# Output weights converted where they are used, and weight splits in front of the products

## The chip, the cores and the metric

One core of a Trainium2 chip runs the whole program. The metric is the device time of one execution in microseconds (us); the median of several executions is compared. TensorE (PE) multiplies, with its weight loads (PEld) on a row of their own, VectorE (DVE), ScalarE (ACT) and GpSimd (POOL) do the rest, and SyncE (SP) issues most transfers.

## The reference

The program is three stages on 2304 tokens (4 batches of 576) with 512 features.

```python
kv = np.einsum('bhsd,bhse->bhde', k, v); out = np.einsum('bhsd,bhde->bhse', q, kv)
x = out / sqrt(mean(out * out, -1) + 1e-6) * g_norm          # linear attention, heads joined
e = argmax(x @ w_gate); gate = softmax(x @ w_gate)[e]        # one of 8 experts, capacity 576
x = gate * (maximum(x @ w1[e], 0) @ w2[e])                   # w1: 512x1024, w2: 1024x512
h = maximum(maximum(x @ m2w1, x @ m2w2), x @ m2w3)           # maxout, 512x768 each
out = h @ w_out                                              # 768x512
```

The four matrices of the maxout stage arrive as doubles (64 bits); everything else is float32.

## The kernel before, in words

**Products.** Every float32 operand of a large product is split into a high part `hi` and a remainder `lo`, and a product is three matmuls (`mm3`, L765 to L767): hi·hi, hi·lo, lo·hi. Here `hi` is written by ScalarE and `lo` by VectorE. For a weight tile of 128x512 this pair stands in `split_next` (L297 on ScalarE, L298 on VectorE); `stream[0]` counts the tiles, and the tile of the w1 chunk f of expert r is t = 16r + f. Weights come into four `raw` buffers of 512 KB, two tiles each; the transfer of a later chunk is asked for when the second half of an earlier one has been split (`raw_upto`).

**Experts.** The experts run one after the other. For expert r, eight groups `gemm1_f` (f = 0 to 7) give `ph`, of which ScalarE writes the high part of `h` (L788, relu) and VectorE its remainder (L789). Then four groups `gemm2_dc` give `py`; the group walks through h 0 to 7 in order, so its first group needs the last `h` some 3 us after it begins. Row counts fall from 374 (second expert) to 284 (eighth); the first expert has 324. In the first expert VectorE also does the ranking of the experts between the products (`rk_gen`).

**Doubles.** Float32 copies of the maxout matrices are made during the experts, in blocks of 128x256 doubles. One `dbl_step` stores block i-3 (transfer queue of ScalarE), loads block i+3 (SyncE) and converts block i in `dbl_round`: two ScalarE instructions (L912, L913), three of VectorE (L914, L915, L917), two of GpSimd (L918, L919). There are 48 blocks: 36 of the three maxout matrices, 12 of the output matrix. `DBL1[r]` lists the f after which a step stands, `DBL2[r][dc]` how many stand after a `gemm2_dc`. Steps past the last block only store. The float32 copies go to DRAM and come back as `raw` chunks.

**Maxout.** The tokens are taken in six blocks of 384 (j). For each of six column chunks c, three products `pa` of 12 matmuls each use six PSUM buffers in turn (three per c). ScalarE copies `pa[0]` to `m` (L1096), VectorE takes the maximum with the other two (L1097, L1098), ScalarE writes the high part of `g` (L1099) and VectorE its remainder (L1100). Then three groups `pz` of 18 matmuls multiply g of c = 0 to 5 with the tiles `wot(c)` of the output matrix. At j = 0 the last maxout tiles (c = 0) and the six output tiles (two each at c = 1, 2, 3) are still to be split; `split_next` stands behind the matmuls of c and ahead of `m`.

**Order.** The schedule is manual: each engine carries out its instructions in the order in which the code writes them.

Of the kernel before, what the change touches and what calls it, by code (L numbers as in the profile page):

```python
# [21 lines left out]
B, H, S, D = 4, 8, 576, 64  # L22
NT, DM, NE, FF, F2 = B * S, H * D, 8, 1024, 768
# [17 lines left out]
def kernel(  # L41
# [21 lines left out]
    ct = dram.tile([NT, 3], F32, name="ct")  # L63

    doubles = []
    if m2w1.dtype == mybir.dt.int64:
        d64 = [m2w1, m2w2, m2w3, m2wo]
        m2w1, m2w2, m2w3 = (dram.tile([DM, F2], F32, name=f"m2w{a}") for a in range(3))
        m2wo = dram.tile([F2, DM], F32, name="m2wo")
        for cb in range(F2 // 256):  # L70
            for a, dst in enumerate([m2w1, m2w2, m2w3]):
                for rb in range(NDC):
                    doubles.append((d64[a], dst, rb, cb))
        for rb in range(NC2):
            for cb in range(DM // 256):
                doubles.append((d64[3], m2wo, rb, cb))
    ND = len(doubles)
# [155 lines left out]
    sp, act = ENG.SP, ENG.Activation  # L233
    NRAW = NE * 8 + 12
    NW = 20
# [12 lines left out]
    def raw_dma(i):  # L248
# [16 lines left out]
        if j < 9:  # L265
# [3 lines left out]
        j -= 9  # L269
        return nc.sync.dma_start(raw.rearrange("p (c f) -> p c f", c=2),  # L270
                                 m2wo[j * 256:(j + 1) * 256, :].rearrange("(c p) f -> p c f", p=128))

# [7 lines left out]

    def split_next(n=1, eng=None):
        for _ in range(n):
            i, half = divmod(stream[0], 2)
            stream[0] += 1
            if i >= NRAW:
                continue
            raw = raws[i]
            t_ = wtile(2 * i + half)
            wt[2 * i + half] = t_
            if i < NE * 8 + 9:  # L290
                src = raw.rearrange("p (c f) -> p c f", c=4)[:, :, half * 128:(half + 1) * 128]
# [610 lines left out]
    def dbl_round(i):  # L902

        if i < ND:
            t_ = dt_[i]
            w_ = dpool[0].tile([128, 256], F32, tag="dw", bufs=6, name=f"dw{i}")
            dt_[i, "w"] = w_
            lo, hi = t_[:, :, 0], t_[:, :, 1]  # L910
            wi = w_.bitcast(I32)
            nc.scalar.activation(out=w_, in_=hi.bitcast(F32), func=AF.Copy, scale=2.0 ** -112)  # L912
            nc.scalar.activation(out=lo.bitcast(F32), in_=lo.bitcast(U32), func=AF.Copy, scale=2.0 ** -52)  # L913
            nc.vector.tensor_scalar(out=wi, in0=wi, scalar1=3, scalar2=None, op0=ALU.logical_shift_left)  # L914
            nc.vector.scalar_tensor_tensor(out=wi, in0=hi, scalar=-2 ** 31, in1=wi,  # L915
                                           op0=ALU.bitwise_and, op1=ALU.bitwise_or)
            nc.vector.tensor_scalar(out=hi, in0=wi, scalar1=-2 ** 23, scalar2=None, op0=ALU.bitwise_and)  # L917
            nc.gpsimd.tensor_tensor(out=lo.bitcast(F32), in0=hi.bitcast(F32), in1=lo.bitcast(F32), op=ALU.mult)  # L918
            nc.gpsimd.tensor_tensor(out=w_, in0=lo.bitcast(F32), in1=w_, op=ALU.add)  # L919

# [107 lines left out]

    DBL1 = [(), (3, 5), (3, 5), (1, 3, 5), (1, 4), (1, 4), (1, 4), (1, 3, 5, 7)]
    DBL2 = [(0, 0, 0, 0), (1, 1, 1, 2), (1, 2, 1, 2), (1, 2, 1, 2), (1, 1, 1, 2)] + [(1, 1, 1, 1)] * 2 + [(2, 2, 0, 0)]  # L1030
    for r in range(NE):
# [10 lines left out]
        if r == NE - 1:  # L1042
            ct_load()
        for f in range(NFC):
            gemm1_f(r, f)
            if r == 0:
                for _ in range(9 if f == 0 else 6):
                    next(rk_gen, None)
                if f == 3:
# [32 lines left out]
    for j in range(NYB):  # L1082
        h2 = []
        for c in range(NC2):
# [36 lines left out]
    with tc.If(flag):  # L1121
        spill(ctx, tc, dict(
            er_f=er_f, nr_f=nr_f, mr_f=mr_f, trir=trir, capf=capf, e2304=e2304, slot=slot, ident=ident, g2=g2,
            xs=xs, ct=ct, w1=w1, w2=w2, m2w=m2w, m2wo=m2wo, out=out))


def spill(ctx, tc, a):
# [3 lines left out]
    with ExitStack() as st:  # L1131
# [164 lines left out]
```

## Time and profile before

| | |
|---|---|
| median of 3 executions (lowest, highest) | 647.64 us (646.8, 650.21) |
| the profiled execution: its time, its span | 650.49 us, 648.6 us |
| TensorE busy | 619.0 us (95%), mean granted clock 0.982 |
| VectorE, ScalarE, GpSimd busy | 338.0, 274.0, 196.5 us |
| attention and routing / experts / maxout, from the timeline | 0 to 88 / 88 to 337 / 337 to 649 us |

The three boundaries are the first matmul of the first expert and the first of the maxout part on TensorE. Busy time of an engine other than TensorE matters only where TensorE waits for it.

### The profile page before, as it was taken

To read this page: it belongs to the slowest core of one execution; us is meant where nothing else is said; L and a number is where in the kernel's file an instruction comes from. 1 tells how busy PE (TensorE), PEld (TensorE's weight loads), DVE (VectorE), ACT (ScalarE), POOL (GpSimd) and SP (SyncE) were. 2 spreads that over 40 slices of the span, in tenths; PEclk is the share of its full clock that TensorE was granted. 3 is DMA by queue.
4 is the path that set the end of the run, shared out by engine and by line. 5 is a ranking of instruction groups with operands and counts; after the bars stand their busy time and mean duration, and the time that the engine had idled before them with its cause. 6 is when DMAs were issued, how large, how long until landed. Compare 5 with 4: busy or idle time off the path is not lost.

```text
span 648.6 us, 11278 instructions
## 1 busy us (share of the span) xinstructions
PE 619.0 (95%) x4113; PEld 593.8 (92%) x4113; DVE 338.0 (52%) x718; ACT 274.0 (42%) x629; POOL 196.5 (30%) x278
## 2 busy tenths in 40 slices
PE   8898988999999999999999999999999999999992
PEld 8788888999998989999999989989989989989992
DVE  2546867886889888888985322222322222221220
ACT  1655864856575857576753221121121121121110
POOL 3247643122858585857530010010010010001001
PEclk9978998999999999999999999999999999999997
DMA  8999347866888788888962000000000000000000
GB/s 226 282 297 297 122 164 236 256 234 214 246 249 276 235 264 254 259 251 255 275 184 65 1 34 16 1 33 17 1 33 17 0 17 33 0 17 33 1 18 35
DMA packets 81373, 88.35 MB, mean 136 GB/s; under 512 B 15017, under 2 KB 70825, under 8 KB 81314
## 3 DMA queue, kind: packets, MB, share of 16 engines
q1 hardware_dynamic: 68448, 66.64, 35.5%
q0 software_dynamic: 5952, 14.65, 6.5%
q10 hardware_dynamic: 6914, 6.30, 2.8%
q8 instruction: 34, 0.56, 0.4%
q14 instruction: 25, 0.20, 0.1%
HBM read 71.80 MB, written 15.76 MB: 135 GB/s over the span
## 4 chain that ended last, share of the span: by engine, by line
PE 63%; DVE 9%; DMA 4%; issue 3%; ACT 2%; ACTq 0%; POOL 0%; SPq 0%; DVEq 0%; POOLq 0%
PE pa L767 12%; PE pa L766 12%; PE pa L765 12%; PE py L766 4%; DVE w L298 4%; PE py L767 4%; PE py L765 4%; PE pz L1110 4%; PE pz L1109 4%; PE pz L1111 4%; DVE h L789 2%; DMA d<-in_moe_w_dram 2%; PE ph L767 2%; PE ph L766 2%; PE ph L765 2%
## 5 line engine op out<-in xcount | busy, mean ns | idle before, releaser
L766 PE MATMUL pa<-ys,w 128*128 128x384 f32 x432 | 144.3, 334 | 0.0
L765 PE MATMUL pa<-ys,w 128*128 128x384 f32 x432 | 144.3, 334 | 0.0
L767 PE MATMUL pa<-ys,w 128*128 128x384 f32 x432 | 144.3, 334 | 0.0
L298 DVE TENSOR_TENSOR w<-raw,w 128x512 fp32r<-128x512 f32 x152 | 114.6, 783 | 26.7 <-ACT w L297 23.1
L1114 POOL DMA_INDIRECT out_dram<-o,ctab x18 | 17.5, 973 | 286.9 <-ACT o L1113 276.7
L1097 DVE TENSOR_TENSOR m<-pa,m 128x384 f32<-128x384 f32 x36 | 20.1, 558 | 137.6 <-PE pa L767 137.6
L297 ACT ACTIVATE w<-raw 128x512 fp32r<-128x512 f32 x152 | 89.5, 624 | 4.8 <-DMA raw<-in_moe_w_dram 4.8
L766 PE MATMUL py<-h,w 128*128 128x324 f32 (+7 forms) x256 | 81.4, 318 | 7.2 <-DVE h L789 7.2
L1099 ACT ACTIVATE g<-m 128x384 fp32r<-128x384 f32 x36 | 18.9, 526 | 150.0 <-DVE m L1098 150.0
L766 PEld LDWEIGHTS pa<-ys,w 128*128 128x128 f32 x432 | 81.1, 188 | 0.2
L765 PEld LDWEIGHTS pa<-ys,w 128*128 128x128 f32 x432 | 81.1, 188 | 0.2
L767 PEld LDWEIGHTS pa<-ys,w 128*128 128x128 f32 x432 | 81.1, 188 | 0.0
L765 PE MATMUL py<-h,w 128*128 128x324 f32 (+7 forms) x256 | 80.2, 313 | 0.0
L767 PE MATMUL ph<-xt,w 128*128 128x324 f32 (+7 forms) x256 | 79.6, 311 | 0.5 <-DVE w L298 0.5
L765 PE MATMUL ph<-xt,w 128*128 128x324 f32 (+7 forms) x256 | 79.3, 310 | 0.6 <-ACT xt L667 0.6
L767 PE MATMUL py<-h,w 128*128 128x324 f32 (+7 forms) x256 | 79.8, 312 | 0.0
L766 PE MATMUL ph<-xt,w 128*128 128x324 f32 (+7 forms) x256 | 79.4, 310 | 0.2 <-DVE xt L668 0.2
L766 PEld LDWEIGHTS py<-h,w 128*128 128x128 f32 x256 | 48.8, 191 | 10.8 <-DVE h L789 10.6
L918 POOL TENSOR_TENSOR d<-d 128x256 f32<-128x256 f32 x48 | 30.7, 640 | 75.5 <-issue 18.2
L765 PEld LDWEIGHTS ph<-xt,w 128*128 128x128 f32 x256 | 48.3, 189 | 0.8 <-ACT xt L667 0.8
L767 PEld LDWEIGHTS ph<-xt,w 128*128 128x128 f32 x256 | 48.3, 189 | 0.8 <-DVE w L298 0.8
L765 PEld LDWEIGHTS py<-h,w 128*128 128x128 f32 x256 | 48.9, 191 | 0.0
(247 smaller groups left out, 1034.1 us busy)
## 6 DMA issues: line engine op xcount, KB each, us to landing
raw<-in_moe_w_dram SPq DMA_DIRECT2D x64, 512.0 KB, 5.4
d<-in_moe_w_dram SPq DMA_DIRECT2D x36, 256.0 KB, 5.2
m2w<-dw ACTq DMA_DIRECT2D x36, 128.0 KB, 4.5
raw<-m2w SPq DMA_DIRECT2D x9, 512.0 KB, 4.6
k<-in_k_dram SPq DMA_DIRECT2D x8, 512.0 KB, 8.7
v<-in_v_dram SPq DMA_DIRECT2D x8, 512.0 KB, 9.2
q<-in_q_dram SPq DMA_DIRECT2D x8, 512.0 KB, 8.5
d<-in_moe_w_out_dram SPq DMA_DIRECT2D x12, 256.0 KB, 5.2
```

The source lines that it names most:

```text
L297: nc.scalar.activation(out=hi, in_=src, func=AF.Copy)
L298: (eng or nc.vector).tensor_tensor(out=lo, in0=src, in1=hi.bitcast(F32), op=ALU.subtract)
L765: nc.tensor.matmul(po, lhi, rhi, start=first, stop=False)
L766: nc.tensor.matmul(po, lhi, rlo, start=False, stop=False)
L767: nc.tensor.matmul(po, llo, rhi, start=False, stop=last)
L918: nc.gpsimd.tensor_tensor(out=lo.bitcast(F32), in0=hi.bitcast(F32), in1=lo.bitcast(F32), op=ALU.mult)
L1097: nc.vector.tensor_tensor(out=m_, in0=pa[1][:, :YB], in1=m_, op=ALU.max)
L1099: nc.scalar.activation(out=t_[:, 0], in_=m_, func=AF.Copy)
L1109: nc.tensor.matmul(po, h_[:, 0], w_[:, 0], start=c == 0, stop=False)
L1110: nc.tensor.matmul(po, h_[:, 0], w_[:, 1], start=False, stop=False)
L1111: nc.tensor.matmul(po, h_[:, 1], w_[:, 0], start=False, stop=c == NC2 - 1)
L1114: nc.gpsimd.indirect_dma_start(out=out, out_offset=IndirectOffsetOnAxis(ap=ctab[:, jt, 0:1].bitcast(I32), axis=0), in_=o_, in_offset=None)
```

## The change

**Output matrix.** Its 12 blocks leave the list of doubles. `raw` now takes 128x512 doubles of it directly, six chunks instead of three. In `split_next` each of the six output tiles is converted first (`to_float32`, the same seven instructions on 512 columns, on a tile `wd`) and then split, at j = 0: one maxout chunk's two tiles at c = 0, two output tiles at c = 1, one each at c = 2 to 5. For a rarely needed branch (`spill`, skipped by a flag in these runs) the split tiles, not float32, are stored to DRAM.

**Schedule of the doubles.** `DBL1` and `DBL2` place 39 steps (36 blocks and three that only store) where 51 stood.

**First expert.** `split_next` stands ahead of `gemm1_f`: four tiles at f = 0, two at f = 1 to 4, none at 5, and one behind the group at f = 6 and 7. Before it stood behind the group, two tiles at f = 0 to 5.

```diff
-        d64 = [m2w1, m2w2, m2w3, m2wo]
+        d64 = [m2w1, m2w2, m2w3]
-        for rb in range(NC2):
-            for cb in range(DM // 256):
-                doubles.append((d64[3], m2wo, rb, cb))
...
-    NRAW = NE * 8 + 12
+    NRAW = NE * 8 + 9 + NC2
...
+    def to_float32(lo, hi, w_):
+        wi = w_.bitcast(I32)
+        nc.scalar.activation(out=w_, in_=hi.bitcast(F32), func=AF.Copy, scale=2.0 ** -112)
+        nc.scalar.activation(out=lo.bitcast(F32), in_=lo.bitcast(U32), func=AF.Copy, scale=2.0 ** -52)
+        nc.vector.tensor_scalar(out=wi, in0=wi, scalar1=3, scalar2=None, op0=ALU.logical_shift_left)
+        nc.vector.scalar_tensor_tensor(out=wi, in0=hi, scalar=-2 ** 31, in1=wi,
+                                       op0=ALU.bitwise_and, op1=ALU.bitwise_or)
+        nc.vector.tensor_scalar(out=hi, in0=wi, scalar1=-2 ** 23, scalar2=None, op0=ALU.bitwise_and)
+        nc.gpsimd.tensor_tensor(out=lo.bitcast(F32), in0=hi.bitcast(F32), in1=lo.bitcast(F32), op=ALU.mult)
+        nc.gpsimd.tensor_tensor(out=w_, in0=lo.bitcast(F32), in1=w_, op=ALU.add)
...
+                src = xgs[0].tile([128, H, D], F32, tag="xn", name=f"wd{i}").rearrange("p h d -> p (h d)")
+                words = raw.bitcast(I32).rearrange("p (f c) -> p f c", c=2)
+                to_float32(words[:, :, 0], words[:, :, 1], src)
             nc.scalar.activation(out=hi, in_=src, func=AF.Copy)
-            (eng or nc.vector).tensor_tensor(out=lo, in0=src, in1=hi.bitcast(F32), op=ALU.subtract)
+            nc.vector.tensor_tensor(out=lo, in0=src, in1=hi.bitcast(F32), op=ALU.subtract)
...
-    DBL1 = [(), (3, 5), (3, 5), (1, 3, 5), (1, 4), (1, 4), (1, 4), (1, 3, 5, 7)]
-    DBL2 = [(0, 0, 0, 0), (1, 1, 1, 2), (1, 2, 1, 2), (1, 2, 1, 2), (1, 1, 1, 2)] + [(1, 1, 1, 1)] * 2 + [(2, 2, 0, 0)]
+    DBL1 = [(), (3, 5, 7), (1, 3, 5, 7), (1, 3, 5, 7), (3, 7), (7,), (), (1, 3, 5)]
+    DBL2 = [(0,) * 4] + [(1,) * 4] * 3 + [(1,) * 4, (1, 1, 1, 0), (1, 1, 1, 0), (0,) * 4]
...
         for f in range(NFC):
+            if r == 0:
+                split_next(4 if f == 0 else 2 if f < 5 else 0)
             gemm1_f(r, f)
...
-            split_next(1 if r else 2 if f < 6 else 0)
+            split_next(1 if r or f > 5 else 0)
...
             if j == 0:
-                split_next(2)
+                split_next(2 if c < 2 else 1)
```

**Where the instructions stand.** ScalarE in the maxout part, from the first block's `m` on. Before, two splits (`w` from `raw`) stand between `g` of one chunk and `m` of the next:

```order
L1096 ACTIVATE m_4864<-pa_4819 128x384
L1099 ACTIVATE g_4865<-m_4864 128x384
L297 ACTIVATE w_4910<-raw_4734 128x512
L297 ACTIVATE w_4913<-raw_4734 128x512
L1096 ACTIVATE m_4916<-pa_4871 128x384
L1099 ACTIVATE g_4917<-m_4916 128x384
L297 ACTIVATE w_4962<-raw_4779 128x512
L297 ACTIVATE w_4965<-raw_4779 128x512
L1096 ACTIVATE m_4968<-pa_4923 128x384
L1099 ACTIVATE g_4969<-m_4968 128x384
```

Now the two converting instructions and the split of each output tile stand there, and the split reads `wd`, which GpSimd finishes:

```order
L312 ACTIVATE w_4726<-raw_4570 128x512
L312 ACTIVATE w_4729<-raw_4570 128x512
L1105 ACTIVATE m_4734<-pa_4687 128x384
L1108 ACTIVATE g_4735<-m_4734 128x384
L283 ACTIVATE wd_4781<-raw_4604 128x512
L284 ACTIVATE raw_4604<-raw_4604 128x512
L312 ACTIVATE w_4780<-wd_4781 128x512
L283 ACTIVATE wd_4795<-raw_4647 128x512
L284 ACTIVATE raw_4647<-raw_4647 128x512
L312 ACTIVATE w_4794<-wd_4795 128x512
L1105 ACTIVATE m_4808<-pa_4741 128x384
L1108 ACTIVATE g_4809<-m_4808 128x384
```

So `m` of chunk 1 stands behind two whole conversions, and `m` of each chunk from 2 on behind one.

VectorE in the fifth expert (314 rows), from the fourth `h` of the first product to the last one. Before (the `dw` and `d` instructions are the conversion of one block):

```order
L789 SCALAR_TENSOR_TENSOR h_3279<-ph_3266,h_3279 128x314
L298 TENSOR_TENSOR w_3282<-raw_3029,w_3282 128x512
L789 SCALAR_TENSOR_TENSOR h_3300<-ph_3287,h_3300 128x314
L298 TENSOR_TENSOR w_3303<-raw_3110,w_3303 128x512
L914 TENSOR_SCALAR dw_3309<-dw_3309 128x256
L915 SCALAR_TENSOR_TENSOR dw_3309<-d_3158,dw_3309 128x256
L917 TENSOR_SCALAR d_3158<-dw_3309 128x256
L789 SCALAR_TENSOR_TENSOR h_3332<-ph_3319,h_3332 128x314
L298 TENSOR_TENSOR w_3335<-raw_3110,w_3335 128x512
L789 SCALAR_TENSOR_TENSOR h_3355<-ph_3342,h_3355 128x314
L298 TENSOR_TENSOR w_3358<-raw_3155,w_3358 128x512
L789 SCALAR_TENSOR_TENSOR h_3376<-ph_3363,h_3376 128x314
```

Now, from the fifth `h` on:

```order
L808 SCALAR_TENSOR_TENSOR h_3289<-ph_3276,h_3289 128x314
L313 TENSOR_TENSOR w_3292<-raw_3110,w_3292 128x512
L808 SCALAR_TENSOR_TENSOR h_3310<-ph_3297,h_3310 128x314
L313 TENSOR_TENSOR w_3313<-raw_3110,w_3313 128x512
L808 SCALAR_TENSOR_TENSOR h_3333<-ph_3320,h_3333 128x314
L313 TENSOR_TENSOR w_3336<-raw_3155,w_3336 128x512
L808 SCALAR_TENSOR_TENSOR h_3354<-ph_3341,h_3354 128x314
L313 TENSOR_TENSOR w_3357<-raw_3155,w_3357 128x512
L285 TENSOR_SCALAR dw_3365<-dw_3365 128x256
L286 SCALAR_TENSOR_TENSOR dw_3365<-d_3113,dw_3365 128x256
L288 TENSOR_SCALAR d_3113<-dw_3365 128x256
```

The conversion that stood among the last four `h` now stands behind the last one. Ahead of that stretch and behind the fourth expert's last `gemm2_dc` group, the number of conversions falls from three to two.

ScalarE at the begin of the first expert, before (`TENSOR_LOAD` and `ISA` read three offsets into registers; `w` are weight splits, `h` the relu of a product):

```order
L297 ACTIVATE w_1291<-raw_697 128x512
L297 ACTIVATE w_1294<-raw_697 128x512
L1024 TENSOR_LOAD po_i
L1024 ISA x2
L1024 TENSOR_LOAD po_i
L1024 ISA x2
L1024 TENSOR_LOAD po_i
L1024 ISA x2
L788 ACTIVATE h_1369<-ph_1356 128x324
L297 ACTIVATE w_1385<-raw_699 128x512
L297 ACTIVATE w_1388<-raw_699 128x512
L788 ACTIVATE h_1406<-ph_1393 128x324
```

And now:

```order
L312 ACTIVATE w_1291<-raw_697 128x512
L312 ACTIVATE w_1294<-raw_697 128x512
L1031 TENSOR_LOAD po_i
L1031 ISA x2
L1031 TENSOR_LOAD po_i
L1031 ISA x2
L1031 TENSOR_LOAD po_i
L1031 ISA x2
L312 ACTIVATE w_1356<-raw_699 128x512
L312 ACTIVATE w_1359<-raw_699 128x512
L312 ACTIVATE w_1364<-raw_701 128x512
L312 ACTIVATE w_1367<-raw_701 128x512
```

The four splits moved ahead of the first `h`, but stay behind the register loads.

## Rows read from the trace of the kernel before

**Rows 1.** The page: busy time by engine.

```profile
PE 619.0 (95%) x4113; PEld 593.8 (92%) x4113; DVE 338.0 (52%) x718; ACT 274.0 (42%) x629; POOL 196.5 (30%) x278
```

**Rows 2.** Waits of the weight loads (PEld), first expert, 94 to 124 us: total, times, longest.

```profile
PEld py L766 <- DVE h L789: 2.6, 2, 1.4
PEld ph L767 <- DVE w L298: 0.8, 1, 0.8
```

**Rows 3.** The same for the fourth to eighth expert, 192 to 337 us.

```profile
PEld py L766 <- DVE h L789: 7.4, 10, 1.3
```

**Rows 4.** The same for the second to eighth expert, 124 to 337 us.

```profile
PEld py L766 <- DVE h L789: 8.0, 11, 1.3
```

**Rows 5.** Busy by stretch (PE, PEld, DVE, ACT, POOL); then granted clock, DMA share, GB/s.

```profile
94.00:110.00 16.00, 13.44 (x84) 12.46 (x83) 15.08 (x49) 8.63 (x19) 5.28 (x4) 0.99 0.60 183
110.00:113.00 3.00, 3.00 (x13) 3.00 (x13) 0.00 (x0) 1.35 (x5) 0.00 (x0) 0.50 0.97 282
337.10:374.55 37.45, 37.45 (x219) 37.45 (x218) 16.92 (x30) 12.25 (x25) 0.00 (x0) 1.00 0.11 35
```

**Rows 6.** Timeline of ScalarE, start of the first expert: start, length, instruction, idle before.

```profile
88.10 1.14 ACT L297 ACTIVATE w<-raw 128x512 fp32r<-128x512 f32 x2
93.42 0.44 ACT L788 ACTIVATE h<-ph 128x324 fp32r<-128x324 f32 x1 [4.18 <-PE ph L767]
```

**Rows 7.** Timeline of VectorE, first expert: first and last two of eight h.

```profile
93.90 0.50 DVE L789 SCALAR_TENSOR_TENSOR h<-ph,h 128x324 fp32r<-128x324 f32 x1 [2.59 <-ACT h L788]
...
108.88 0.89 DVE L789 SCALAR_TENSOR_TENSOR h<-ph,h 128x324 fp32r<-128x324 f32 x2
```

**Rows 8.** Timeline of TensorE, begin of the first expert's second product.

```profile
107.81 0.42 PE L766 MATMUL py<-h,w 128*128 128x324 f32 x1 [1.16 <-DVE h L789]
...
109.42 0.54 PE L766 MATMUL py<-h,w 128*128 128x324 f32 x1 [0.90 <-DVE h L789]
...
110.29 0.47 PE L766 MATMUL py<-h,w 128*128 128x324 f32 x1
```

**Rows 9.** Timeline of VectorE near the end of the fourth expert's first product.

```profile
208.07 1.44 DVE L298 TENSOR_TENSOR w<-raw,w 128x512 fp32r<-128x512 f32 x1
```

**Rows 10.** Source line L297, split, ScalarE: minimum/median/maximum ns, first and last start.

```profile
L297 ACT ACTIVATE w<-raw x152: 613/623/650, 84.5 to 357.6; 128x512 fp32r<-128x512 f32 x152
```

**Rows 11.** Source line L298, split, VectorE, the same columns.

```profile
L298 DVE TENSOR_TENSOR w<-raw,w x152: 675/691/1441, 85.2 to 358.3; 128x512 fp32r<-128x512 f32 x152
```

**Rows 12.** Source line L912, conversion, ScalarE.

```profile
L912 ACT ACTIVATE dw<-d x48: 421/428/443, 134.8 to 329.1; 128x256 f32<-128x256 f32 x48
```

**Rows 13.** Source line L914, conversion, VectorE.

```profile
L914 DVE TENSOR_SCALAR dw<-dw x48: 279/286/1062, 135.8 to 331.3; 128x256 int32<-128x256 int32 x48
```

**Rows 14.** Source line L915, conversion, VectorE.

```profile
L915 DVE SCALAR_TENSOR_TENSOR dw<-d,dw x48: 424/426/920, 136.1 to 331.6; 128x256 int32<-128x256 int32 x48
```

**Rows 15.** Source line L917, conversion, VectorE.

```profile
L917 DVE TENSOR_SCALAR d<-dw x48: 294/296/796, 136.6 to 332.1; 128x256 int32<-128x256 int32 x48
```

**Rows 16.** Source line L918, conversion, GpSimd.

```profile
L918 POOL TENSOR_TENSOR d<-d x48: 610/615/1059, 137.0 to 332.6; 128x256 f32<-128x256 f32 x48
```

**Rows 17.** Source line L919, conversion, GpSimd.

```profile
L919 POOL TENSOR_TENSOR dw<-d,dw x48: 739/1064/1114, 137.7 to 333.6; 128x256 f32<-128x256 f32 x48
```

**Rows 18.** Groups by line and form: a 512-column GpSimd instruction; busy, mean ns, idle before.

```profile
L516 POOL TENSOR_TENSOR orow<-ohl,rnorm 128x512 f32<-128x512 f32 x12 | 12.1, 1033 | 0.0
```

**Rows 19.** Timeline of ScalarE in the maxout part, first block.

```profile
344.13 0.53 ACT L1099 ACTIVATE g<-m 128x384 fp32r<-128x384 f32 x1 [2.72 <-DVE m L1098]
344.56 1.14 ACT L297 ACTIVATE w<-raw 128x512 fp32r<-128x512 f32 x2
345.62 0.49 ACT L1096 ACTIVATE m<-pa 128x384 f32<-128x384 f32 x1
```

**Rows 20.** Timeline of VectorE in the maxout part, first block.

```profile
343.54 0.56 DVE L1098 TENSOR_TENSOR m<-pa,m 128x384 f32<-128x384 f32 x1 [1.07 <-PE pa L767]
```

**Rows 21.** Timeline of TensorE: the sixteenth matmul of the first output product.

```profile
378.03 0.40 PE L1109 MATMUL pz<-w,g 128*128 128x512 f32 x1
```

More of the change, by code (lines that the diff above doesn't have):

```diff
@@ L66 @@
     if m2w1.dtype == mybir.dt.int64:
-        d64 = [m2w1, m2w2, m2w3, m2wo]
+        d64 = [m2w1, m2w2, m2w3]
         m2w1, m2w2, m2w3 = (dram.tile([DM, F2], F32, name=f"m2w{a}") for a in range(3))
-        m2wo = dram.tile([F2, DM], F32, name="m2wo")
+        m2wos = dram.tile([F2, 2, DM], F32, name="m2wos")
         for cb in range(F2 // 256):
@@ L269, in raw_dma @@
         j -= 9
-        return nc.sync.dma_start(raw.rearrange("p (c f) -> p c f", c=2),
-                                 m2wo[j * 256:(j + 1) * 256, :].rearrange("(c p) f -> p c f", p=128))
+        return nc.sync.dma_start(raw.bitcast(I32), m2wo[j * 128:(j + 1) * 128, :].bitcast(I32))
     stream, issued, ready = [0], [0], [8]
@@ L279, in raw_upto, with split_next @@
             issued[0] += 1
-    def split_next(n=1, eng=None):
+    def to_float32(lo, hi, w_):
[8 more added lines that the diff above has]
+        nc.gpsimd.tensor_tensor(out=w_, in0=lo.bitcast(F32), in1=w_, op=ALU.add)
+    def split_next(n=1):
         for _ in range(n):
-            i, half = divmod(stream[0], 2)
+            t = stream[0]
             stream[0] += 1
-            if i >= NRAW:
+            if t >= NT1 + 18 + NC2:
                 continue
+            i = t // 2 if t < NT1 + 18 else NE * 8 + 9 + t - NT1 - 18
             raw = raws[i]
-            t_ = wtile(2 * i + half)
-            wt[2 * i + half] = t_
+            t_ = wtile(t)
+            wt[t] = t_
             if i < NE * 8 + 9:
+                half = t % 2
                 src = raw.rearrange("p (c f) -> p c f", c=4)[:, :, half * 128:(half + 1) * 128]
@@ L293, in split_next @@
             else:
-                src = raw[:, half * 512:(half + 1) * 512]
-                hi = t_[:, 0].rearrange("p c f -> p (c f)")
-                lo = t_[:, 1].rearrange("p c f -> p (c f)")
-            nc.scalar.activation(out=hi, in_=src, func=AF.Copy)
-            (eng or nc.vector).tensor_tensor(out=lo, in0=src, in1=hi.bitcast(F32), op=ALU.subtract)
+                half = 1
+                hi, lo = (t_[:, x].rearrange("p c f -> p (c f)") for x in range(2))
+                src = xgs[0].tile([128, H, D], F32, tag="xn", name=f"wd{i}").rearrange("p h d -> p (h d)")
+                words = raw.bitcast(I32).rearrange("p (f c) -> p f c", c=2)
+                to_float32(words[:, :, 0], words[:, :, 1], src)
+            nc.scalar.activation(out=hi, in_=src, func=AF.Copy)
+            nc.vector.tensor_tensor(out=lo, in0=src, in1=hi.bitcast(F32), op=ALU.subtract)
+            if i >= NE * 8 + 9:
+                c0 = (i - NE * 8 - 9) * 128
+                nc.sync.dma_start(m2wos[c0:c0 + 128].rearrange("p s f -> p (s f)"),
+                                  t_.bitcast(F32).rearrange("p s c f -> p (s c f)"))
             if half == 1:
@@ L909, in dbl_round @@
             dt_[i, "w"] = w_
[L910 to L919, printed above, removed]
+            to_float32(t_[:, :, 0], t_[:, :, 1], w_)
     def dbl_store(i):
@@ L1123 @@
             er_f=er_f, nr_f=nr_f, mr_f=mr_f, trir=trir, capf=capf, e2304=e2304, slot=slot, ident=ident, g2=g2,
-            xs=xs, ct=ct, w1=w1, w2=w2, m2w=m2w, m2wo=m2wo, out=out))
+            xs=xs, ct=ct, w1=w1, w2=w2, m2w=m2w, m2wos=m2wos, out=out))
 def spill(ctx, tc, a):
@@ L1191, in spill @@
         wo = wpool.tile([128, NC2, DM], F32, name="sp_wo")
-        nc.sync.dma_start(wo, a["m2wo"].rearrange("(c p) f -> p c f", p=128))
+        wl = wpool.tile([128, NC2, DM], F32, name="sp_wl")
+        for i, w_ in enumerate((wo, wl)):
+            nc.sync.dma_start(w_, a["m2wos"].rearrange("(c p) s f -> s p c f", p=128)[i])
+        V.tensor_tensor(out=wo, in0=wo, in1=wl, op=ALU.add)
         def ps(nm):
```

## The prediction

> **What bounds the kernel now.** The page comes first: TensorE is busy for 619.0 us [rows 1] of a span of 648.6 us, VectorE for half of it. So time is won only where TensorE waits, and lost only where it is made to. The list of TensorE's waits, cut by stage, is next, for the weight loads, since they reach a missing operand first. In the first expert they wait 2.6 us in two places for `h` of VectorE, and 0.8 us for a weight split [rows 2]. In the fourth to eighth expert it is 7.4 us in ten places, always for `h`, always at the begin of the second product [rows 3]; with the second and third expert it is 8.0 us in eleven places [rows 4]. In the maxout part TensorE is busy without a gap, while GpSimd does nothing and ScalarE and VectorE are busy for 12.25 and 16.92 of 37.45 us [rows 5]. The reader is to see two facts: the stage that is relieved has at most some 11 us to give, and the stage that takes the work has idle engines but a TensorE without slack.
>
> **Fourth to eighth expert: what is removed.** VectorE is late with the last `h` because weight splits and conversions stand among them. Counting conversions from the last group of the expert before to the last `h`: five before and four now in the fourth expert, four and two in the fifth, four and one in the sixth, three and none in the seventh, four and none in the eighth, whose three steps only store. One conversion costs VectorE 0.28 + 0.43 + 0.30 us at the medians [rows 13 to 15], and the maxima beside them (1.06, 0.92, 0.80) and a split of 1.44 us [rows 9] against a median of 0.69 [rows 11] show what GpSimd's share costs it on top. The longest single wait is 1.3 us [rows 3], so two conversions less end it. Only the fourth expert, with one less for 2.1 us of waits in two places, may keep some 0.4. I take 7.0 us off. Bounds: nothing less than 3 us, if only the plain 1.0 us per conversion counted and other work moved up; at most 8.0, if the second expert's wait went too [rows 4]. The second and third expert have as many conversions ahead of the last `h` as before, and no change is counted.
>
> **First expert: splits ahead of the products.** The register loads that read three offsets keep ScalarE from its first `h` until 93.42 us, 4.18 us after its last split [rows 6], and they still stand ahead of the moved splits. So the moved splits begin at 93.42, too, their VectorE halves 0.66 us later. From 93.90 to the end of the eighth `h` at 109.77 [rows 7] VectorE has no gap worth the name (15.08 of 16.0 us busy [rows 5]), and it has the same work to do in another order, plus one split (0.60 to the next instruction, 1.28 for two) that now stands ahead of the eighth `h`. The eighth `h` then ends at 94.08 + 15.87 + 0.60 = 110.55, the seventh at 109.5, the sixth at 109.1, the fifth at 108.4. The split wait of 0.8 us goes, since the fifth to eighth tiles are ready by 96.5, but TensorE only reaches the second product sooner and waits there. Before, the seventh `h` let it go at 109.42 and its array was at the lower of its two clocks, 1.2 instead of 2.4 GHz, up to 113 (0.50 granted [rows 5]): from 109.42 three matmuls further to 110.29 [rows 8], 0.29 us each. Now it goes on with the fifth `h` at 108.4, and three `h` later, at that lower clock, it reaches the eighth at 108.4 + 9 × 0.28 = 110.9, where it was at 110.29 before [rows 8]: **0.6 us lost**. Bounds: 4.9 us won, if all waits (3.4) and the lower clock (1.5) went, for which VectorE would have to have less to do; 2.5 lost, if the lower clock lasted twice as long. I take 0.6, since VectorE's work is the same.
>
> **Maxout part: what is added.** The seven instructions of a conversion follow one another over three engines, and ScalarE carries both ends: the first copy, and the split that waits for GpSimd's sum. `m` of the same chunk stands behind that split. So per output tile ScalarE is held for a time k:
>
> - first copy 0.62 (a 512-column split [rows 10]; 0.43 at 256 [rows 12]),
> - VectorE 0.41 + 0.69 + 0.43: at 256 columns 0.28, 0.43, 0.30; the middle one grows to a 512-column split's 0.69 [rows 11], the two short ones by half as much, 0.13,
> - GpSimd 1.03 + 1.16: a 512-column instruction takes 1.03 [rows 18], 0.42 more than the multiply's 0.61 [rows 16]; the add's minimum 0.74 [rows 17] plus the same 0.42, the minimum because VectorE is idle meanwhile,
> - the split 0.52 until ScalarE can go on (two in 1.14 [rows 19]), and some 0.42 for six hand-overs, an estimate from gaps of 0.03 to 0.13 between these lines.
>
> That is k = 5.3 us. Between `m` and the next conversion ScalarE needs E = 2.25: VectorE's split (0.60), two maxima (0.56 each, 0.50 to the next), `g` (0.43 to the next), hand-overs [rows 19, 20]. A chunk of TensorE takes 37.45 / 6 = 6.24 us [rows 5], so from chunk 2 on ScalarE needs 7.55 and falls behind by 1.3 per chunk, and chunk 1 has two conversions. Two sets of PSUM buffers hide this at first; then `pa` of chunks 4 and 5 and the first `pz` wait about 1.3 us each, and the rest at `pz`'s sixth chunk. The sum is easier from the end. Conversions begin at 344.56 [rows 19]; `m` of chunk 5 begins at 344.56 + 6k + 4E, its `g` ends 2.35 later, at 355.9 + 6k. TensorE needs it at 378.03 [rows 21]. The delay is **6k - 22.1 = 9.7 us**. Bounds: at the 256-column prices as they stand k is 3.7 and the delay 0.3; with every length doubled and the add at its median of 1.06, k is 7.2 and the delay 21. I keep near the middle since fixed and per-column parts both show in [rows 16, 18].
>
> The last wait, over 5 us, should leave the array at the lower clock for a while, as two waits of 1.16 and 0.90 us did before 110 us [rows 8]: 3.0 us at a granted 0.50 [rows 5], **1.5 us**. The Trainium skill (TensorE: Matmul & The Clock Gate, "Part 1: The HAM clock gate") has the array fall back to half rate once it has been idle, and return only after sustained work; by that alone the waits of 1.3 us between busy chunks would cost no clock, and the sum stays as it is. The row speaks for less tolerance: if each of the three shorter waits cost 1.5 as well, the sum would be 4.5 higher, a rival below.
>
> Added at no cost: six 512 KB loads and six 512 KB stores, since DMA is 11% busy in this stretch [rows 5] and nobody waits for the stores but the next load on SyncE, three tiles ahead; without that cover TensorE would wait for a load's landing. Twelve loads, stores and reloads of the old path vanish from queues that TensorE does not wait for.
>
> **Sum.** -7.0 + 0.6 + 9.7 + 1.5 = +4.8 us on the profiled execution's 650.49 (a span of 648.6 and 1.9 around it), that is 655.3, or 0.74%. The median of the runs shown is 647.64, 0.4% below that execution; the same 4.8 us on it give **652.4**. About 0.5% (3.2 us) is what a measurement of this kernel can tell from no change.
>
> **Rivals.**
>
> - *The conversions are hidden* (other side, 0.15): ScalarE and VectorE are idle for more than half of the stretch, and if k is below 4.1 the delay is under 2.5 us and the clock stays up: 647.64 - 7.0 + 0.6 + 0.3 to 2.5, so 641.5 to 643.8. The whole change breaks even at k = 4.5. For it: two engines idle; against it: idle time does not help a chain in which ScalarE waits in its own queue.
> - *Longer chain, or the lower clock at each wait* (0.19): k of 6 (4.2 more) or four falls of the clock (4.5 more), or both: 656.6 to 661.
> - *The first expert gives its 4.9 us* (0.10): 652.4 - 5.5 = 646.9, no change. For it: TensorE meets no missing weight tile; against it: VectorE's full queue [rows 5, 7].
> - *The experts' waits stay by half*, because GpSimd's indirect transfers or the splits keep VectorE late (0.08): 3.5 less is won, 655.9.
>
> **How the numbers follow.** My forecast has 0.48. Its own range is 649.5 to 656, k from 4.8 to 5.9. A sixth of it (0.08) lies within 0.5%. Slower: 0.40 + 0.19 + 0.08 = 0.67; within 0.5%: 0.08 + 0.10 + 0.02 of the first rival = 0.20; faster: 0.13. The range leaves out most of the first rival and the far end of the second: 644.5 to 661.
>
> **What would show it.** Right: in the first maxout block ScalarE's `m` of chunk 1 starts some 11 us after `g` of chunk 0, TensorE waits at `pa` and longest at the first `pz` for `g`, some 10 us in sum, with the granted clock falling after it; in the fourth to eighth expert the waits for `h` are under 1 us in sum; in the first expert they are no smaller than now. Wrong: TensorE without gaps in the first maxout block, so k under 4; or waits for `h` still in the sixth to eighth expert.

## The result, and the profile after

The changed kernel takes 652.23 us (median of 19 runs, 649.58 to 654.84), the kernel before 648.04 us in 19 runs on the same chip: a ratio of 1.0066, 95% interval 1.0047 to 1.0085. That is 4.2 us more, where 4.8 were forecast (652.4 us).

The profiled execution of after has a span of 648.5 us, which hardly differs from the 648.6 of before, and this is the first thing to clear up. The kernel's time is cut here into stages by the first matmul of each (`ph`, the first product of an expert; `pa`, the first block of the maxout part), read from TensorE's timeline:

| stage | before, us | after, us | difference |
|---|---|---|---|
| up to the first product of the first expert | 88.26 | 84.35 | -3.9 |
| first and second expert | 35.43 + 34.31 | 33.48 + 34.58 | -1.7 |
| third expert | 31.91 | 31.92 | 0.0 |
| fourth to eighth expert | 147.2 | 139.6 | -7.6 |
| first maxout block, with its second part | 50.0 | 63.1 | +13.1 |
| the next four blocks, 49.98 each | 199.9 | 199.9 | 0.0 |
| the last block, to the end of the span | 61.6 | 61.6 | 0.0 |

The stretch ahead of the first product holds no instruction that the change moves, and it varies from execution to execution: among the fourteen profiles of this study it is 82 to 98 us long. One of the fourteen, that of late_first_old_2, is of a slow execution (654.06 us, 643.29 at that kernel's fastest) and isn't used. Without its 3.9 us the stages add up to +3.8 us, close to the 4.2 of the runs.

**The maxout part.** TensorE, without a gap here before [rows 5], now waits four times, always for ScalarE. The list of waits of TensorE's matmuls from 324 to 388 us (us in total, times, longest):

```profile
PE pz L1118 <- ACT g L1108: 6.1, 1, 6.1
PE pa L784 <- ACT m L1105: 2.6, 2, 1.3
PE pz L1118 <- ACT m L1105: 1.3, 1, 1.3
```

TensorE's timeline has them one by one (start, duration, and in brackets the idle time ahead and what ended it): `pa` of chunks 4 and 5, the first `pz`, and the sixth chunk of `pz`.

```profile
350.63 0.45 PE L784 MATMUL pa<-ys,w 128*128 128x384 f32 x1 [1.30 <-ACT m L1105]
...
358.48 0.44 PE L784 MATMUL pa<-ys,w 128*128 128x384 f32 x1 [1.32 <-ACT m L1105]
...
366.31 0.50 PE L1118 MATMUL pz<-w,g 128*128 128x512 f32 x1 [1.30 <-ACT m L1105]
...
376.16 0.80 PE L1118 MATMUL pz<-w,g 128*128 128x512 f32 x1 [6.09 <-ACT g L1108]
```

One turn of ScalarE shows why. Its timeline for chunk 2 reads: two copies of the conversion (L283, L284), the split that waits 3.66 us for GpSimd's sum (L312), only then `m` (L1105) and `g`, then the next conversion.

```profile
344.69 0.65 ACT L283 ACTIVATE wd<-raw 128x512 f32<-128x512 f32 x1
345.25 0.67 ACT L284 ACTIVATE raw<-raw 128x512 f32<-128x512 uint32 x1
349.57 0.63 ACT L312 ACTIVATE w<-wd 128x512 fp32r<-128x512 f32 x1 [3.66 <-POOL wd L290]
350.11 0.47 ACT L1105 ACTIVATE m<-pa 128x384 f32<-128x384 f32 x1
352.09 0.53 ACT L1108 ACTIVATE g<-m 128x384 fp32r<-128x384 f32 x1 [1.51 <-DVE m L1107]
352.52 0.66 ACT L283 ACTIVATE wd<-raw 128x512 f32<-128x512 f32 x1
```

From the first copy to `m` it is 350.11 - 344.69 = 5.42 us (k, forecast 5.3), from `m` to the next conversion 352.52 - 350.11 = 2.41 (E, forecast 2.25). A turn is 7.83 us and TensorE's chunk 6.24, so TensorE loses 7.83 - 6.24 = 1.6 us with each chunk as soon as its PSUM buffers are used up. The list shows 1.3 of it: it counts the time in which the array is idle, and matmuls that otherwise overlap (0.33 us long, 0.17 from start to start) do not overlap across a wait. GpSimd's two instructions in the chain, by line and shape (count, busy us, mean ns; from 336 to 376 us, which leaves out the first of six multiplies), are the largest piece of k:

```profile
L290 POOL TENSOR_TENSOR wd<-raw,wd 128x512 f32<-128x512 f32 x6 | 7.8, 1302 | 0.5
L289 POOL TENSOR_TENSOR raw<-raw 128x512 f32<-128x512 f32 x5 | 5.2, 1040 | 24.7 <-DVE raw L288 13.9 <-issue 10.8
```

The granted clock after the waits, by windows (the second-last columns are the granted clock and the DMA share): the 2 us behind the third wait are at full clock, as are those behind the first two; the 3.9 us behind the wait of 6.1 us are at the lower one.

```profile
366.40:368.40 2.00, 2.00 (x9) 1.65 (x10) 1.30 (x4) 0.63 (x2) 0.00 (x0) 1.00 0.50 207
376.16:380.06 3.90, 3.90 (x10) 3.09 (x11) 2.41 (x5) 2.29 (x5) 1.02 (x1) 0.52 0.10 38
380.06:384.06 4.00, 4.00 (x19) 3.25 (x18) 0.00 (x0) 0.69 (x1) 0.00 (x0) 1.00 0.18 70
```

**The experts.** TensorE's weight loads waited 7.4 us in ten places for `h` in the fourth to eighth expert [rows 3]. After, the list from 152 us to the maxout part is empty, and from 110 us on it holds one wait for `h`, in the second expert:

```profile
PEld ph L785 <- DVE xt L698: 0.6, 1, 0.6
PEld py L785 <- DVE h L808: 0.6, 1, 0.6
```

**The first expert** looks unlike [rows 2] and [rows 5]: the second product's waits for `h` are 0.7 us in place of 2.6, with 0.5 for `off_f`, and the lower clock lies at its begin, not at its end. The windows are the 6 us ahead of the first product, the first 6 us of it, and the 10.8 us behind them.

```profile
PEld py L785 <- DVE h L808: 0.7, 2, 0.5
PEld py L785 <- DVE off_f L899: 0.5, 1, 0.5
```
```profile
78.35:84.35 6.00, 5.37 (x31) 5.15 (x31) 2.32 (x6) 2.00 (x5) 5.12 (x11) 0.60 0.54 175
84.35:90.35 6.00, 6.00 (x23) 5.69 (x24) 3.32 (x8) 2.93 (x6) 0.68 (x1) 0.55 0.52 198
90.35:101.17 10.82, 10.82 (x75) 10.82 (x75) 10.23 (x38) 7.67 (x17) 3.95 (x4) 1.00 0.74 214
```

Whether the new order did that, or the clock that this execution had before the change begins, one profile can't tell.

### The profile page after: what moved, and what is told of

It reads as the page before. It is cut to its first block, busy times and chain, and to the rows that moved or that the text cites. A ratio compares the mean times of both kernels' runs of the same rounds, so it can differ in the third digit from the quotient of the medians.

```text
span 648.5 us, 11170 instructions
## 1 busy us (share of the span) xinstructions
PE 614.8 (95%) x4113; PEld 590.4 (91%) x4113; DVE 328.4 (51%) x700; ACT 273.6 (42%) x617; POOL 193.3 (30%) x266
## 5 line engine op out<-in xcount | busy, mean ns | idle before, releaser
L313 DVE TENSOR_TENSOR w<-raw,w 128x512 fp32r<-128x512 f32 x146 | 106.8, 759 | 32.4 <-ACT w L312 29.1
L312 ACT ACTIVATE w<-raw 128x512 fp32r<-128x512 f32 x146 | 86.1, 623 | 6.1 <-issue 3.1
L785 PE MATMUL py<-h,w 128*128 128x324 f32 (+7 forms) x256 | 79.5, 310 | 0.8 <-DVE h L808 0.5
L784 PE MATMUL py<-h,w 128*128 128x324 f32 (+7 forms) x256 | 79.6, 311 | 0.0
L786 PE MATMUL py<-h,w 128*128 128x324 f32 (+7 forms) x256 | 79.2, 310 | 0.0
L1118 PE MATMUL pz<-w,g 128*128 128x512 f32 x108 | 43.6, 403 | 7.4 <-ACT g L1108 6.1
L785 PEld LDWEIGHTS ph<-xt,w 128*128 128x128 f32 x256 | 49.1, 192 | 1.0 <-DVE xt L698 0.6
L785 PEld LDWEIGHTS py<-h,w 128*128 128x128 f32 x256 | 48.3, 189 | 1.8 <-DVE h L808 1.3
L784 PEld LDWEIGHTS ph<-xt,w 128*128 128x128 f32 x256 | 49.1, 192 | 0.9 <-ACT xt L686 0.9
L786 PEld LDWEIGHTS ph<-xt,w 128*128 128x128 f32 x256 | 49.2, 192 | 0.0
```

The lines of the kernel that those rows point to most:

```text
L313: nc.vector.tensor_tensor(out=lo, in0=src, in1=hi.bitcast(F32), op=ALU.subtract)
L784: nc.tensor.matmul(po, lhi, rhi, start=first, stop=False)
L785: nc.tensor.matmul(po, lhi, rlo, start=False, stop=False)
L786: nc.tensor.matmul(po, llo, rhi, start=False, stop=last)
L1118: nc.tensor.matmul(po, h_[:, 0], w_[:, 0], start=c == 0, stop=False)
```

## The experiments

Times are compared by the ratio to the kernel before on the same chip, since that kernel took 648.3, 656.2 and 657.0 us on the three chips that were used.

**The chain taken out of ScalarE's queue (split_late).** The same instructions, but the split of an output tile, with VectorE's half and the store, stands behind `g` of the next chunk, and the next conversion behind it, so that `m` never stands behind a split that waits. (The function `split_late` itself is left out below; it holds the split, VectorE's half, the store and the request for the next load.)

```diff
                 to_float32(words[:, :, 0], words[:, :, 1], src)
+                late.append((i, t_, hi, lo, src))
+                continue
...
             if j == 0:
-                split_next(2 if c < 2 else 1)
+                if c == 0:
+                    split_next(3)
...
             nc.vector.tensor_tensor(out=t_[:, 1], in0=m_, in1=t_[:, 0].bitcast(F32), op=ALU.subtract)
+            if j == 0:
+                split_late()
+                split_next(1)
```

> The changed kernel with the same work in another order: a tile of output weights is converted in one chunk of the maxout part, but its split stands behind g of the next chunk, so m of a chunk no longer stands behind a split that waits for GpSimd. Theory (a chain over three engines in ScalarE's queue): TensorE's waits in the first maxout block (11.2 us in the profile after) fall below 1 us and the lower clock behind them (1.8 us) goes, so 652.2 - 13 = 639 us (638 to 641), 9 us below the kernel before. Rival (the amount of work on ScalarE, VectorE and GpSimd, or the loads and stores, hold TensorE up): half or more of the waits stay, 645 us or more.

Measured: 638.31 us, ratio 0.9866 [0.9825, 0.9907], and on two other chips 0.9868 [0.9840, 0.9896] and 0.9831 [0.9802, 0.9861]. It beats both kernels, by some 9 us and 13 us. TensorE is busy without a gap again in the first block and its second part, in windows:

```profile
324.74:362.18 37.44, 37.44 (x219) 37.44 (x217) 23.41 (x43) 16.88 (x33) 13.75 (x12) 1.00 0.39 141
362.18:374.71 12.53, 12.53 (x55) 10.14 (x55) 3.65 (x7) 4.09 (x8) 2.42 (x3) 1.00 0.17 66
```

ScalarE's timeline now has the split (L323) right behind `g` with no wait, and `m` (L1115) behind the copies:

```profile
344.25 0.53 ACT L1118 ACTIVATE g<-m 128x384 fp32r<-128x384 f32 x1 [3.67 <-DVE m L1117]
344.68 0.61 ACT L323 ACTIVATE w<-wd 128x512 fp32r<-128x512 f32 x1
345.20 0.66 ACT L283 ACTIVATE wd<-raw 128x512 f32<-128x512 f32 x1
345.76 0.66 ACT L284 ACTIVATE raw<-raw 128x512 f32<-128x512 uint32 x1
346.33 0.47 ACT L1115 ACTIVATE m<-pa 128x384 f32<-128x384 f32 x1
```

The work is all there: over the whole span VectorE is busy for 329.4 us and ScalarE for 272.9, after for 328.4 and 273.6. So the rival, that the amount of work or the transfers hold TensorE up, falls; what cost 13.1 us is the place of one split in one queue.

**A shorter chain (sum_on_vector).** For the six output tiles the multiply and the add run on VectorE.

```diff
-        nc.gpsimd.tensor_tensor(out=lo.bitcast(F32), in0=hi.bitcast(F32), in1=lo.bitcast(F32), op=ALU.mult)
-        nc.gpsimd.tensor_tensor(out=w_, in0=lo.bitcast(F32), in1=w_, op=ALU.add)
+        eng = nc.vector if w_.shape[-1] == 512 else nc.gpsimd
+        eng.tensor_tensor(out=lo.bitcast(F32), in0=hi.bitcast(F32), in1=lo.bitcast(F32), op=ALU.mult)
+        eng.tensor_tensor(out=w_, in0=lo.bitcast(F32), in1=w_, op=ALU.add)
```

> The changed kernel with the multiply and the add of the six output tiles on VectorE in place of GpSimd. Theory (chain): GpSimd's 1.04 + 1.30 us and their hand-overs, 2.4 us, become two VectorE instructions of 0.65, so each of six tiles holds ScalarE 1.1 us less and the waits fall by 6 x 1.1 = 6.6, from 11.2 to 4.6 us; the total 652.2 - 6.6 = 645.6 us (643.5 to 646.5, the lower end if the lower clock goes too). Rival (the amount of VectorE's work decides): VectorE has 8 us more to do and the waits stay or grow, 652 us or more.

Measured: 645.19 us, ratio 0.9974 [0.9946, 1.0002]. The first block with its second part takes 56.8 us in place of 63.1: 6.3 less, against 6.6 expected; k is 4.41 us there (first copy at 342.14, `m` at 346.55), 1.01 less. One wait is left, of TensorE's matmuls from 322 to 402 us:

```profile
PE pz L1119 <- ACT g L1109: 5.1, 1, 5.1
```

More work on VectorE made it faster, as the chain explains and the rival does not. The Trainium skill (Perfetto Trace Analysis, "Optimizing GPSIMD Operations") prefers other engines where possible; this run agrees, with 6.3 us for twelve instructions.

**A longer chain (sum_twice).** One more add on GpSimd in each of the six conversions, into a place that nobody reads.

```diff
+        if w_.shape[-1] == 512:
+            nc.gpsimd.tensor_tensor(out=hi.bitcast(F32), in0=lo.bitcast(F32), in1=w_, op=ALU.add)
         nc.gpsimd.tensor_tensor(out=w_, in0=lo.bitcast(F32), in1=w_, op=ALU.add)
```

> The changed kernel with one more add of 1.30 us on GpSimd in each output tile's conversion, whose result goes unused, so that the chain that holds ScalarE is longer by 1.38 us with the hand-over. Theory (chain, six times its length): the waits in the first maxout block grow from 11.2 to 11.2 + 6 x 1.38 = 19.5 us, the short ones from 1.5 to 2.9 us each, and the lower clock behind the longest costs 1.9 as before: 652.2 + 8.3 = 660.5 us. Rival (the array falls to the lower clock at each of the short waits too, now that they are longer): 1.5 us more for each of three or four, 665 to 666.5 us. Other rival (the chain is not what is waited for): 652.2 us.

Measured: ratio 1.0196 [1.0163, 1.0228], that is 1.0129 times the changed kernel's ratio, or 8.4 us; the stage takes 71.4 us, 8.25 more (8.3 expected), and k is 6.83 us (355.48 to 362.31), 1.41 more. The total follows the chain. The waits (of TensorE's matmuls, 322 to 420 us) do not look as expected, though:

```profile
PE pz L1120 <- ACT g L1110: 7.5, 1, 7.5
PE pa L786 <- ACT m L1107: 6.6, 3, 2.8
PE pz L1120 <- ACT m L1107: 1.1, 1, 1.1
```

Their sum is 15.2 us, not 19.5 (this list has 10.0 in after, where the expectation took 11.2). In the timeline they are 2.77, 1.13, 2.67, 1.13 and 7.45 us. The windows from the end of the first, second and third of them on:

```profile
353.59:357.59 4.00, 4.00 (x16) 4.00 (x17) 3.23 (x7) 1.67 (x3) 0.00 (x0) 0.70 0.71 255
362.83:366.83 4.00, 4.00 (x23) 4.00 (x24) 3.23 (x7) 1.66 (x3) 0.00 (x0) 1.00 0.32 131
372.04:376.04 4.00, 4.00 (x14) 4.00 (x15) 3.22 (x7) 1.69 (x3) 0.00 (x0) 0.57 0.33 133
```

Behind the waits of 2.77 and 2.67 us the array was at its lower clock for part of the 4 us, behind the 1.13 not. The second rival is right that the clock falls, and wrong that it costs: the chunk that ran slower came to the next operand later, and its wait was shorter by about as much (behind the third wait 2.67 - 1.13 = 1.5 us, against the 0.43 x 4 = 1.7 us that a granted 0.57 takes from 4 us). While the chain sets the pace, TensorE's clock is hidden behind it.

**The conversions' places among the experts (late_old_table).** The reordered kernel with the tables of the kernel before, so that its 36 conversions stand in the old density up to the sixth expert.

```diff
-    DBL1 = [(), (3, 5, 7), (1, 3, 5, 7), (1, 3, 5, 7), (3, 7), (7,), (), (1, 3, 5)]
+    DBL1 = [(), (3, 5), (3, 5), (1, 3, 5), (1, 4), (1, 4), (1, 4), (1, 3, 5, 7)]
```

(and `DBL2` likewise)

> The reordered kernel with the two tables of the kernel before, so that its 36 conversions stand as densely as before until the sixth expert and none is left from then on. Theory (VectorE is late with the last h because of the conversions among them): the fourth, fifth and sixth expert take 32.4, 31.0 and 29.4 us again in place of 30.7, 28.9 and 27.6, with waits for h, the seventh and eighth stay at 26.8 and 25.6; 5.7 us more in all, 644.0 us (642.5 to 645). Rival (what relieved these experts is the smaller number of loads, stores and conversions as such, not their places): no wait comes back, 638.3 us.

Measured: 32.70, 30.77 and 29.48 us for the fourth to sixth expert, 26.79 and 25.59 for the seventh and eighth; ratio 0.9935 [0.9910, 0.9960] beside 0.9868 on the same chip, (0.9935 - 0.9868) x 656.2 = 4.4 us more (5.7 expected, within what the two intervals leave open). In the profiles the fourth to sixth expert take 92.9 us, 87.2 in split_late_again, which is the 5.7 expected. The waits of the weight loads in these experts are back in six places:

```profile
PEld py L794 <- DVE h L817: 4.7, 6, 1.3
PEld py L794 <- DVE d L288: 0.8, 1, 0.8
```

So the place of the steps, not their number, makes the last `h` late. A step is a store, a load and a conversion; no run took these three apart.

**The first expert's order, alone and undone (first_old, first_only, late_first_old).** The edit, forward or back, is the same in the kernel after, the one before and the reordered one:

```diff
         for f in range(NFC):
+            if r == 0:
+                split_next(4 if f == 0 else 2 if f < 5 else 0)
             gemm1_f(r, f)
...
-            split_next(1 if r else 2 if f < 6 else 0)
+            split_next(1 if r or f > 5 else 0)
```

> The changed kernel with the first expert's splits behind the products again, as before. Theory A (the prediction's step: VectorE's work is the same, the new order costs 0.6 us): 651.6 us, and the waits of TensorE for h and a split in the first expert come back at no loss. Theory B (the profile after, in which the first expert takes 33.7 us in place of 35.4): 1.7 us slower than the changed kernel, 653.9 us. Theory C (the new order gives all of the waits and the lower clock back): 4.9 us slower, 657 us.

> The kernel before with only the first expert's splits moved ahead of the products. Theory A (0.6 us lost): 648.6 us; first expert 35.4 + 0.6 = 36.0 us from its first product to the second expert's first. Theory B (1.7 us won): 646.3 us, first expert 33.7 us. Theory C (4.9 us won): 643.1 us, first expert 30.5 us. All with the conversions of before, so the waits of the fourth to eighth expert (7.4 us) stay and the maxout part has none.

> The reordered kernel with the first expert's splits behind the products, as in the kernel before. Theory A (VectorE's work is the same, so the order of the splits alone changes nothing; the 2 us less in the profile of the changed kernel came from the clock that its array happened to have): first expert 35.5 us at the full clock, total 638.3 us within 1.2. Theory B (the splits in front gain 1.7 to 2 us): 640.2 us.

Measured: first_old 1.0063 [1.0036, 1.0090] (the changed kernel 1.0066); first_only 0.9971 [0.9942, 1.0001]; late_first_old 0.9898 [0.9867, 0.9930], beside 0.9868 [0.9840, 0.9896] with the new order. That is 0.0, 0.3 and 0.3% for the new order, none of it clear of its interval. C falls; between A and B nothing is decided: in first_old B's 653.9 us (1.0090) lies at the end of the interval, in first_only A's 648.6 (1.0009) just beyond it. The lengths of the first two experts in the profiles tell more. The first ones seemed to follow the clock before the first product. Of the next five texts the first belongs to the run beside late_first_old on the second chip (0.9868, and at a granted 0.50 a first expert of 33.79 us); the other four are of a third chip:

> The reordered kernel (split behind g of the next chunk) once more, to stand on the same chip beside the next two. Every theory: 638.3 us within 1.2. If the array is at the lower clock before the first product in this execution, the first expert takes 33.5 us (as in the profile of the changed kernel), else 35.5 us (as in the reordered kernel's first profile).

> The reordered kernel a third time, new order of the first expert's splits. Theory D (what the new order is worth hangs on the clock before the first product): first and second expert together take 69.6 to 70.4 us if the granted clock in the 6 us before the first product is 1.00, 68.0 to 68.6 us if it is 0.50. Theory A (the order is worth nothing) and theory B (it is worth 2 us) allow no such difference between the two orders.

> The reordered kernel with the old order of the first expert's splits, a second time. Theory D: the first two experts take 69.6 to 70.4 us at a granted 1.00 before the first product (as the new order does), and about 70.9 us at 0.50 (2.5 us more than the new order). Theory A: as the new order in either case, so 68.3 us at 0.50. Total 0 to 2.5 us above the new order's.

> The kernel before, unchanged, for another profile of it. Theory D: the first two experts take 69.6 to 70.4 us at a granted 1.00 before the first product and about 70.9 us at 0.50. Theory A: 68.3 us at 0.50. Total as the kernel before.

> The changed kernel with the old order of the first expert's splits, a second time. Theory D: the first two experts take 69.6 to 70.4 us at a granted 1.00 before the first product and about 70.9 us at 0.50. Theory A: 68.3 us at 0.50. Total as the changed kernel's or up to 2.5 us more, 13 us of it again in the first maxout block.

On the third chip the ratios were 0.9831 (split_late_3), 0.9862 [0.9822, 0.9901] (late_first_old_2), 0.9989 [0.9960, 1.0017] (before_2) and 1.0057 [1.0031, 1.0083] (first_old_2); for the new order in the reordered kernel that is 0.3% again. The first two experts in the profiles, in us:

| order | kernel | granted clock, 6 us ahead of the first product | first expert | second | both |
|---|---|---|---|---|---|
| old | before | 1.00 | 35.43 | 34.31 | 69.7 |
| old | first_old | 1.00 | 35.59 | 34.02 | 69.6 |
| old | before_2 | 1.00 | 33.32 | 37.86 | 71.2 |
| old | first_old_2 | 0.50 | 32.76 | 36.87 | 69.6 |
| old | late_first_old | 0.50 | 32.76 | 38.13 | 70.9 |
| new | split_late | 1.00 | 35.50 | 34.88 | 70.4 |
| new | split_late_3 | 1.00 | 34.95 | 33.80 | 68.8 |
| new | sum_on_vector | 1.00 | 35.57 | 34.00 | 69.6 |
| new | late_old_table | 1.00 | 36.26 | 33.78 | 70.0 |
| new | after | 0.60 | 33.48 | 34.58 | 68.1 |
| new | first_only | 0.50 | 33.49 | 34.51 | 68.0 |
| new | split_late_again | 0.50 | 33.79 | 34.76 | 68.6 |
| new | sum_twice | 0.50 | 33.61 | 34.88 | 68.5 |

Theory D was read off the rows of the earlier chips, so only the third chip's rows test it, and it misses all three: before_2 (71.2 at 1.00) and split_late_3 (68.8 at 1.00), where 69.6 to 70.4 was expected, and first_old_2 (69.6 at 0.50), where 70.9 was. It falls. What parts the rows better, seen only afterwards and tested by no further run, is the first expert's length. Where it is long, 35 us, the orders are alike; these are the six rows in which the granted clock fell to 0.50 near the begin of the second product, 19 to 21 us into the expert. Where it is short, 33 us, the old order loses 3 us in the second expert, and the new one does not. The means are 70.2 and 69.0 us, 1.2 us for the new order, with ranges that overlap.

The second expert of first_old_2 shows the loss. ScalarE's timeline there: a split waits 1.88 us for a raw weight tile to land, and `h` behind it comes late.

```profile
131.43 0.46 ACT L807 ACTIVATE h<-ph 128x374 fp32r<-128x374 f32 x1
133.77 0.63 ACT L312 ACTIVATE w<-raw 128x512 fp32r<-128x512 f32 x1 [1.88 <-DMA raw<-in_moe_w_dram]
...
135.96 0.47 ACT L807 ACTIVATE h<-ph 128x374 fp32r<-128x374 f32 x1
```

VectorE's half of that split waits with it, 1.65 us. From there to the eighth `h` VectorE has one more gap, of 0.13 us, so the delay reaches that `h` whole, and the weight loads wait for it (list from 127 to 165 us):

```profile
134.44 0.69 DVE L313 TENSOR_TENSOR w<-raw,w 128x512 fp32r<-128x512 f32 x1 [1.65 <-ACT w L312]
...
149.53 0.53 DVE L808 SCALAR_TENSOR_TENSOR h<-ph,h 128x374 fp32r<-128x374 f32 x1
```
```profile
PEld py L785 <- DVE h L808: 2.3, 2, 1.5
```

In the new order, split_late_again at the same place, the landing holds ScalarE 0.16 us, and no weight load of the second product waits for `h`:

```profile
132.21 0.49 ACT L816 ACTIVATE h<-ph 128x374 fp32r<-128x374 f32 x1
132.86 0.63 ACT L314 ACTIVATE w<-raw 128x512 fp32r<-128x512 f32 x1 [0.16 <-DMA raw<-in_moe_w_dram]
...
135.05 0.46 ACT L816 ACTIVATE h<-ph 128x374 fp32r<-128x374 f32 x1
```

## Why the prediction was right

- *Maxout part, 9.7 us of waits and 1.5 us of clock:* the stage is 13.1 us longer, of which (1 - 0.52) x 3.9 = 1.9 are clock and 11.2 the waits (10.0 us in the list, which leaves out the overlap that matmuls lose at a wait). The mechanism, the places and the order of the waits are as forecast; k was 0.12 and E 0.16 short, which makes 6 x 0.12 + 4 x 0.16 = 1.4 us. Nearly all of k's error is GpSimd's add: 1.30 us where I took 1.16 from its minimum at 256 columns. That the short waits read 1.3 us, as forecast, is luck in part: 7.55 - 6.24 = 1.3 was to be lost per chunk, 1.6 was lost, and the list shows 1.3 of that. split_late, sum_on_vector and sum_twice show the cause and its slope, -6.3 and +8.25 us where six times the change of k (from 5.42 to 4.41 and to 6.83) gives -6.1 and +8.5.
- *The shorter waits cost no clock:* so it was in the kernel after, at 1.3 us each. The Trainium skill (TensorE: Matmul & The Clock Gate, "Part 1: The HAM clock gate") has the array fall back only once it has been idle and return after sustained work; the trace agrees for waits of 1.3 us, and in sum_twice those of 2.7 us were followed by the lower clock.
- *Fourth to eighth expert, 7.0 us off:* 7.6 us, all waits gone; the fourth expert kept nothing of the 0.4 that I left it. late_old_table shows that the places of the steps decide. The size rests on one pair of profiles; in the two others with the tables of before these experts take 149.1 us (before_2) and 146.9 (first_only), 9.6 and 7.4 more than after.
- *First expert, 0.6 us lost:* the step about VectorE is borne out, by its timelines. With the array at the lower clock before the first product, the eighth `h` ends 114.78 - 94.38 = 20.4 us after it in the old order (first_old_2; 20.4 in late_first_old) and 116.36 - 95.20 = 21.2 in the new one (split_late_again; 21.2 after), 0.8 later; and the first expert alone is 0.7 to 1.0 us longer there. The sign that the waits there would be no smaller than now did not come in the profile of after (0.7 and 0.5 us, where `h` and a weight split had cost 2.6 and 0.8). It did come in executions of the new order with the array at full clock before the first product: 1.0 for `h` and 2.4 for `off_f` in split_late, 3.1 for `h` in late_old_table. At 0.50 the old order waits less, too (1.5 for `h` in first_old_2).
- *Second expert, no change counted:* this failed. I priced the two splits more only as VectorE's work; splits that run earlier also free raw buffers earlier, and in executions with a short first expert ScalarE's wait for a landing tile in the second one is 1.7 to 2.1 us in the old order (before_2, first_old_2, late_first_old), and 0 to 1.04 in the new (sum_twice, split_late_again, first_only, after). Together -1.2 us in the means (-1.7 in the one pair of profiles), inside my bounds of -4.9 to +2.5, with the sign uncertain. SyncE's loads of `raw` do wait for splits: in first_old_2 13.7 us in nine places from 105 to 136 us, for `w` of VectorE. That early splits shorten the landing waits by starting loads sooner is argued from these rows; no experiment took the loads apart from the splits.
- *The sum:* -7.6 - 1.7 + 13.1 = +3.8 in the profiles, +4.2 in the runs, +4.8 forecast; terms off by -0.6, -2.3 and +1.9 us cancelled in part.

## What to carry to other kernels

Before work is moved to engines that are idle, write down their queues: an instruction that ends a chain over three engines holds everything behind it in its queue, and a loop with it costs (chain + rest - the bound engine's period) each round, here 5.42 + 2.41 - 6.24 = 1.6 us, however idle the engines are. Splitting the chain, its begin in one round and its end behind the next round's urgent work, cost nothing here and turned 4 us of loss into 9 us of gain. And count a moved instruction's buffer too: when it runs sets when the next load may start.

## What was not expected of the hardware

- The lower clock can be free: in sum_twice the array ran at a granted 0.57 over 4 us, and the stage grew by 8.25 us where six times the chain's growth gives 8.5.
- No length of one wait parts the clock's two levels in these rows: 1.3 us alone was followed by 1.00, 2.67 and 2.77 us by the lower clock, but so were the 1.16 and 0.90 us close together before [rows 5, 8]. And the same pair of waits at the same place was not followed by it in the next profile of the same kernel, before_2, of which these are the waits and the 4 us behind them. So the row from which the prediction priced its 1.5 us of clock is one outcome of two.

```profile
108.53 0.42 PE L766 MATMUL py<-h,w 128*128 128x324 f32 x1 [1.17 <-DVE h L789]
...
110.14 0.42 PE L766 MATMUL py<-h,w 128*128 128x324 f32 x1 [0.89 <-DVE h L789]
```
```profile
110.20:114.20 4.00, 4.00 (x27) 4.00 (x28) 1.21 (x3) 2.00 (x6) 0.00 (x0) 1.00 0.85 270
```

- GpSimd's multiply of 128 x 512 took 1.04 us and its add 1.30 (L289 and L290 above), the same shapes and types, in six instances each. The multiply reads and writes every second word of `raw`, while one operand of the add and its result lie dense in `wd`; no run took the operation and the layout apart.
